# Other buffers' times in a planner, a shared first unit, and a new order of work, in a kernel that mixes a gated unit with a long convolution

## The chip, the cores and the metric

The kernel runs on one core of a Trainium2 chip. The core has a matrix engine (PE in the profile; PEld are its weight loads), a vector engine (DVE), a scalar engine (ACT), a general engine (POOL) and SyncE (SP), which here only issues transfers. Transfers (DMA) move data between the chip's large memory and the on-chip buffer; matmuls write their results into eight small banks, from which DVE and ACT read. Every engine works its own list of instructions in order, and waits where an instruction needs what another engine or a transfer has not finished.

The metric is the device time of one execution in microseconds (us), the median of the runs. A forecast of "no change" means within 0.2%, about 1.25 us here.

## The reference

`x` is 2048 rows by 512 channels. Two branches are computed from it and mixed row by row by a gate:

```python
g = sigmoid((x * gate_w).sum(-1, keepdims=True))
# branch a: a convolution over the 2048 rows, one kernel K per channel, from 128 complex modes
P = exp(dt * A [:, :, None] * l);  K = einsum("dn,dnl,dn->dl", C, P, dt * B).real
a = irfft(rfft(x padded to 4096) * rfft(K padded to 4096))[:2048] + x * Dskip
# branch b: a gated unit, 512 -> 1792 -> 512
b = (sigmoid(x @ w_gate) * (x @ w_up)) @ w_down
out = g * a + (1 - g) * b
```

## The kernel before

**Branch b** is most of the matmul work. The rows are worked in two halves of 1024, each half in two blocks (`sb`) of 512 rows; the 1792 columns in 14 tiles (`f`) of 128, and the tiles in four groups of 3, 4, 4 and 3. Each number is split in two parts, a rounded one (written by ACT, L868) and what is left (written by DVE, L869), and three products of parts stand for one product of full precision. One *unit* (`hidden`) is one `f` for one block: a gate matrix (`k` = 0) and an up matrix (`k` = 1), each with 4 slices (`dc`) of the 512 channels times 3 products, so 12 matmuls of 128x512 into one bank `gups`, 24 in a unit. Sigmoid (ACT), product (DVE) and a split follow (`post`); `down` multiplies by w_down into banks `dps`, three matmuls for each `f`. In the first half the weights are split once and written back to memory (`wsp<-gu`, `wsp<-dnw`), and in the second half they are read from there (`gu<-wsp`, 1 MB; `dnw<-wsp`, 512 KB). Sums over groups are added in memory-to-buffer transfers that POOL issues (`acc<-part`).

**Branch a** is made of many small matmuls. `rows` reads x (`u`), computes the gate, and takes the first step of the transform of x: matmuls `ups`, stored as `a_u`. `steps` computes dt = exp(log_dt) for all channels with 22 small DVE instructions (L326 to L347) on the tile `steps`; `preludes` (tiles `dt`, `pg`), `bases` and `tables` build on DVE and ACT the tables `T` and `B` for 16 groups of 32 channels; their product (`kps`, 64 matmuls that the profile counts as 128) is K. Its transform (`wps`) is evacuated by ACT to `kev` and stored as `a_k`, by 256 channels each (`a_k0`, `a_k1`). Then `passes` runs over frequencies: for each 256 channels eight passes, each of which loads a table `wwu`, then `au<-a_u` and `ak<-a_k` (two transfers of 256 KB each, in short pieces), multiplies (`s2u`, `s2k`; `ustep`, `kstep`), forms the complex product on DVE, multiplies back (`ips`; `inverse`) with a table `wwv`, evacuates to `ev` and stores it (`b_s<-ev`). After the eighth pass `finals` reads `b_s` back (`b_in`) for the last step (`fps`; `last`).

**The early buffers.** Constants and `rows` use a pool of buffers called early: among them `wu`, `gwb`, `steps`, the row tiles, and three of the eight staging buffers `st` (the list `more`), through which all split data comes. When `rows` is done this pool is closed, and the buffers of the passes (pool `fin`: `wwu`, `wwv`, `big` for `au` and `ak`, `uf`, `t`, `ev`, `al`) take the same place in the on-chip memory. An instruction that writes such a buffer waits on the chip until the last user of what lay there is done.

**What sets the order.** Nothing is scheduled by the hardware. Each of the parts above is a Python generator that yields the next piece of work, and `Plan.run` interleaves them into one list. The string `ORDER` tells whose turn it is, a letter for each piece (letter h, for instance, is "hidden PE"); a turn that is not ready is owed and taken as soon as it is. What is ready, and which of several free buffers is taken, follows from the plan's own estimates of time: `Plan.cost` for engines; for a transfer by SP the size at 280 KB a us, a fixed part, and a slack (`SLACK["dma"]`, 1.6 us). A `Slot` is a buffer with the time at which the plan holds it free, an `Ev` an event with such a time. These numbers order the work and choose buffers; the waits on the chip follow from the data.

Around the change stand these lines:

- L323 loads log_dt into `steps`; L316 is every constant's load (`pw`, `gwb`, `wu` and others); L864 loads a piece of x (`st<-xt`) or of weights (`st<-wgu`, `st<-wdn`), L868 and L869 split it.
- L947 are the matmuls of `hidden`, L999 those of `down`, L688, L713 and L751 are `s2u`, `s2k` and `ips`.
- L653, L658, L667 and L671 load `wwu`, `au`, `ak` and `wwv`; L766 stores `b_s`.
- `first_w` is a pair of events that make the loads of the first unit take turns: x's slice 0, the gate weights, x's slices 1 to 3, and only then the up weights.

Of the kernel before, what the change touches and what calls it, by code (L numbers as in the profile page):

```python
# [31 lines left out]
P = 128  # L32
L, D, F, NS = 2048, 512, 1792, 128
NM = L // P
NF = F // P
NC = D // P
# [23 lines left out]
    "HJ0zKI56HJzKHJKh4HJhKIQI56hhhhh8zHI56IhhhIHij0JKHQH56ihhJK56h3h3JK569JijKj2hh7ij1y2VVyWPhQh8ijOhhU8VhNijhi9UMPj9UkUyLUVR"  # L60
    "kklhPURhiYOg7YIh5ffikNMIYY6YYjkPLRPONghgklhYhRjgMTg5ikkPLPhVik7VWTIY56hhUYVTjlhUIihkhUkkYYYUYjiYRYONRMPLP3OYN5MPUZIyLTSX"
    "jlkkRhjVTU6iIYgk6PYOhYh55hYbceQNYTYSfj7fgihglRjkaig8kbMkYb!jIhgVlVhiP6YLWUhhhbTPONbVYYkYY9Y5UYYYZi6kMPUTRRUhjILUVPXkj3hh"
    "T!UYi7lOTjY5iYYgYIfjYYfYhRbRNkgTIg7gcYkhQij8hMPe9LPO6kYQ5hgijTRR5hViT6ablhYNbh8hVWbUMPYTbLVhiPkONhhYUYYMTjh!RUYP9kZjXUUT"
    "ViL6UYgRkijjYhhbcQ89kf2Peh!dT6fggOYg1lkkkkgRRiajNlkkYkkib2YYVhbIhhiYMPIVh5YlbkkW5UT6YVbYLUTPONMUPUYRTYL6UYYYYhojRRVoUk7k"
    "IlIRZXbjiYg5fhckjekh7PkYYYkflaoYkYYkohk5YYikYggghbgbhbblVVWU7kI5jhhYiVihUYYYYkYkUUkUoTjIjZXTlk6hiVU6iYh5gffYYjdkIhYYQO8k"
    "Yh6YNMPLYhihhPONRYRjhgiggbgVjVWUk9TMhioYj!yPLhhQ8VYIPcl9eiTRRaYONYk6hh!jQ89!YUQYMih8jTkUbYZXUiPUjjb9iVjb7UYk!YkgLYbYTY5P"
    "lIShYbcfkShkY6hYkefgggkg35oIaYViOoh5lkkVWUk5N6MPT7khIbbVh!7YYhUbiTlkkYYkYYYZLUU6jX6SUVbj5bkl6U!cehYg3RhijkkY2fkhYY12ofTg"
    "YkYlgagkkokkihilkokgdYIboVYYhVbkbWk56UbhVhYYlk!ohUiYUjkToYYjHkYUQUYj8oVkiT9lUZhXQ8jYhgJYYhYQ87bcikYYf9YeaYKHfjog9bbhTkhb"
    "kghibJgl7hHgoJkYVVWkHkYhiUYVlkYojYkKYhYIhYjZUUdpppppUKhUVhpJijiXKQjUCbkYglnYIABBsqppppkYphhceHrYkrHfrfggikrabGYgYhbbjbhY"
    "DEYIYpEhEgVijCHVYWEFJKHABBisqlrhnFprpJhkkUpkVphoprJrihjGUjUDhUnYYYhCKEloEkkJUkYoEYKEFABBYsVUZliqrX!kk3bYgpkYiKp!YrcFfYhe"  # L70
    "rhphjaplfkirYkgYoYpbpjhg3bGbjbDpEEEgYEhCgVVWiiABBQsqrFUVhklrYppprUhFYppQhIhirGYYkUDCEEEYEpFjYhdjjUABYBsqUkrkiiYrnjhpoplV"
    "rFUZhXYbghjY2YhfhckYrYekfYiakYgg12YbgpYlGpgbYhnVbbkVkk!lYDCEpEEYphkkiWUVYAnjEFBBsYFqUiYklpphphjUkpYoZrrprkkrUlXkbckUVGIj"
    "nkUYYDEYgpYYYEEEhlFFYCABnBsqrppYphrkferkpkYfggrpgijIlihahbbGhjbkbDEEEgECphVYAVWYiYUVYiBBUsqrrrQhFhhhrkiUjYFhUQdUYQYGDEEj"
    "EkjhEVijFFUZXYghijhIhbcelYhkfaYYYYYYfYYgYtijYtxkgbithbugtxwubwQhvwhYgYVhvttxtYtxwiwVWUVIwhbYjhiUjZhUvwjvuuijXUtihjhUtxkt"
    "VUYYbklugYYfhvvwwwtvtkYkYYkYYkhfggxhvgwglkktkijVYVkuvxluYvkWUovwwiwkkIcevVtvvokhholYiUoakjUYjkbkYiYYZjbhktUxUVluvUXkkkbk"
    "vbYgYhYYhbYYhYYhYffcYoiYYgeaYgYglkYkgkYIkdbbbbhjhZIliXbkceQokQabbbhbijhjijkdppppphhChihhhjihjihhABBsqprklrrphkpppphppikh"
    "QrGDEpECEpjihEjApBBsqQFhppkhihjrrrrGDiECEEppEjIhjFABBisjqrhohklhkippppokrkrprFpGCDEhEFEpEABBpsqrrrklhkkkwoFjioFCpprABBpI"
    "sjGpqrrrklhirpkpkkpklDEEEpppEpGphpkDEEEEkkpCABBFFsqrrkjrhlIkpkoCApBrBsqGikklrrrhjrphGDEEEEFFpkkkDEoEkplpECEhoABBFsqrihkh"
    "kkrrrjihiFwGDFhFQhhjEEjEEklhhQkkiQFFtjhttijxtxhhkuwutwtthhtvvxxiiwwttwtowtvwjxvohhikktxtxujtuuvvuvvwmkwkkkjotxkkikwkvmuu"
    "jkmwvnnmnvijkkkknmvwwwmknkkkvnwkvvmnvwkmn")  # L80

XLATE = 0
SLACK = dict(dma=1.6, eng=0.06)
FETCH = 6.5

# [184 lines left out]
def body(ctx, tc, xp, xt, prm, ldt, dsk, gw, wgu, wdn, c_wu, c_wf, c_wk, c_wwu, c_wwv, c_pw, out):  # L270
# [573 lines left out]
    def load_x():  # L844
        for half in range(2):
            for sb in range(2):
# [264 lines left out]
```

## Time and profile before

| what | value |
|---|---|
| median of 3 runs | 626.07 us (624.86 to 626.09) |
| the profiled execution: its own time | 625.42 us |
| its span, first to last instruction | 623.7 us |
| PE busy | 608.8 us, 98% |
| DVE busy | 506.4 us, 81% |
| ACT busy | 429.4 us, 69% |
| idle time of PE: 623.7 - 608.8 | 14.9 us |
| moved by DMA | 140.34 MB, 225 GB/s on average |

A row of a timeline is: start and duration in us, engine, line, operation, output<-inputs, shapes, how many instructions were merged into the row, and in brackets how long the engine had been idle and what ended that. A row of the view by stretches gives, for each stretch of time, its length, the busy time of each engine with the number of instructions, the granted clock, the mean busy share of the 16 DMA engines, and the rate in GB/s. The page's "40 slices" cut the span into 40 equal parts of 15.6 us, each digit a busy share in tenths.

### The profile page before, as it was taken

Reading aid. Unit: us, or ns where it says so; the run is one execution under the profiler, and the core shown is the slowest. Engines: PE = TensorE matmul, PEld = TensorE weight load, DVE = VectorE, ACT = ScalarE, POOL = GpSimd, SP = SyncE. Lnnn points to the kernel's source line nnn. Section 1 sums busy time; section 2 is a strip of 40 time slices with the busy share of each in tenths; the row PEclk is TensorE's granted clock in tenths of the full one; section 3 lists DMA queues with packets and bytes.
Section 4 is the critical chain, followed back from the end, with each engine's and each line's share of the span. In section 5 each row is a group of like instructions: output and inputs, shape, how many; then the busy total and the mean of one; then the engine's idle time right before and its main releaser. Section 6 shows DMA issues by size and latency. Waiting matters only on the chain.

```text
span 623.7 us, 16354 instructions
## 1 busy us (share of the span) xinstructions
PE 608.8 (98%) x6816; PEld 461.0 (74%) x6816; DVE 506.4 (81%) x902; ACT 429.4 (69%) x726; POOL 35.1 (6%) x44
## 2 busy tenths in 40 slices
PE   5999999999999999999999999999999999998997
PEld 3877777787777778877776777777787776775775
DVE  5879899999999999999999999998986163663145
ACT  5597988989989798988878687767684233342210
POOL 0000000010100111010110000000201000110000
PEclk9999999999999999999999999999999999999999
DMA  7844866588759498698999678777856999999875
GB/s 226 287 161 122 288 204 200 182 234 272 219 158 292 134 295 255 197 294 239 209 261 281 202 214 211 244 236 227 236 151 180 229 224 264 247 231 235 256 224 178
DMA packets 97161, 140.34 MB, mean 225 GB/s; under 512 B 40000, under 2 KB 65472, under 8 KB 92480
## 3 DMA queue, kind: packets, MB, share of 16 engines
q1 hardware_dynamic: 91328, 128.81, 67.9%
q0 software_dynamic: 5760, 10.49, 10.1%
q8 instruction: 54, 0.88, 0.6%
q14 instruction: 19, 0.16, 0.1%
HBM read 75.31 MB, written 53.48 MB: 207 GB/s over the span
## 4 chain that ended last, share of the span: by engine, by line
PE 87%; DVE 6%; DMA 3%; ACT 1%; SPq 1%; issue 1%; DVEq 0%; ACTq 0%
PE gups L947 45%; PE dps L999 23%; PE kps L527 5%; PE wps L555 3%; PE ups L606 3%; PE fps L801 2%; PE s2u L688 2%; PE s2k L713 2%; PE ips L751 2%; DMA b_s<-ev 1%; DMA ak<-a_k 1%; DMA st<-wgu 1%; SPq L658 1%; DVE uf L725 0%; DVE tt L724 0%
## 5 line engine op out<-in xcount | busy, mean ns | idle before, releaser
L947 PE MATMUL gups<-x,gu 128*128 128x512 f32 x1344 | 332.6, 396 | 7.5 <-ACT gu L868 6.5
L947 PEld LDWEIGHTS gups<-x,gu 128*128 128x128 f32 x1344 | 250.7, 189 | 76.8 <-issue 12.7
L999 PE MATMUL dps<-dnw,h 128*128 128x512 f32 x672 | 175.9, 397 | 0.0
L999 PEld LDWEIGHTS dps<-dnw,h 128*128 128x128 f32 x672 | 123.1, 188 | 35.2 <-issue 9.0
L1024 POOL DMA_DIRECT2D acc<-part x40 | 34.9, 871 | 549.6 <-ACT part L1022 365.9
L970 ACT ACTIVATE h<-sg 128x512 fp32r<-128x512 f32 x56 | 34.9, 627 | 28.5 <-DVE sg L966 28.5
L477 ACT ACTIVATE B<-B 128x32 f32<-128x32 f32 (+2 forms) x96 | 53.3, 669 | 0.4
L971 DVE TENSOR_TENSOR h<-sg,h 128x512 fp32r<-128x512 f32 x56 | 38.3, 685 | 17.7 <-ACT h L970 17.7
L724 DVE TENSOR_TENSOR tt<-s2k,uf 128x512 f32<-128x512 f32 x32 | 21.9, 686 | 35.2 <-PE s2k L713 34.7
L461 DVE TENSOR_TENSOR T<-T,t 128x64 f32<-128x64 f32 (+4 forms) x80 | 46.5, 581 | 1.2
L459 DVE TENSOR_TENSOR t<-T,bz 128x64 f32<-128x64 f32 (+4 forms) x80 | 46.1, 576 | 1.2
L460 DVE TENSOR_TENSOR T<-T,bz 128x64 f32<-128x64 f32 (+4 forms) x80 | 46.2, 577 | 0.0
L966 DVE TENSOR_TENSOR sg<-gups,sg 128x512 f32<-128x512 f32 x56 | 38.0, 683 | 9.5 <-PE gups L947 5.8
L1022 ACT ACTIVATE part<-dps,omg 128x512 f32<-128x512 f32 x40 | 27.4, 684 | 23.6 <-PE dps L999 23.4
L297 ACT ACTIVATE ev<-ips 128x256 f32<-128x256 f32 x64 | 20.0, 387 | 33.4 <-PE ips L751 20.9
L964 ACT ACTIVATE sg<-gups 128x512 f32<-128x512 f32 x56 | 33.6, 601 | 13.2 <-PE gups L947 12.9
L565 ACT ACTIVATE kev<-wps 128x256 f32<-128x256 f32 x64 | 34.8, 643 | 5.6 <-PE wps L555 5.6
L527 PEld LDWEIGHTS kps<-B,T 128*32 128x32 f32 x2048 | 29.4, 110 | 7.4 <-issue 5.0
L527 PE MATMUL kps<-B,T 128*32 128x64 f32 x2048 | 31.9, 220 | 0.3 <-DVE T L461 0.2
L297 ACT ACTIVATE uf<-s2u 128x512 f32<-128x512 f32 x32 | 17.4, 595 | 18.6 <-PE s2u L688 18.5
L430 ACT ACTIVATE af<-ex 128x1216 int32<-128x1216 f32 x16 | 19.6, 1228 | 15.0 <-DVE ex L421 13.4
L431 DVE TENSOR_TENSOR ex<-ex,af 128x1216 f32<-128x1216 f32 x16 | 22.7, 1418 | 0.7 <-ACT af L430 0.5
(85 smaller groups left out, 684.0 us busy)
## 6 DMA issues: line engine op xcount, KB each, us to landing
wsp<-gu SPq DMA_DIRECT2D x14, 1024.0 KB, 6.9
gu<-wsp SPq DMA_DIRECT2D x14, 1024.0 KB, 7.7
acc<-part POOLq DMA_DIRECT2D x40, 256.0 KB, 6.0
a_u<-evu SPq DMA_DIRECT2D x32, 256.0 KB, 4.4
a_k<-kev SPq DMA_DIRECT2D x8, 1024.0 KB, 5.0
au<-a_u SPq DMA_DIRECT2D x32, 256.0 KB, 6.0
ak<-a_k SPq DMA_DIRECT2D x32, 256.0 KB, 6.7
b_s<-ev SPq DMA_DIRECT2D x32, 256.0 KB, 4.1
```

What stands on the lines that cost most here:

```text
L297: copy = lambda eng, out_, in_: A.activation(out_, in_, AF.Copy) if eng == "ACT" else V.tensor_copy(out_, in_)
L459: yield "DVE", dve(n), lambda: V.tensor_tensor(t2, src, sb, op=OP.mult), [t, slot.t]
L460: t = yield "DVE", dve(n), lambda: V.tensor_tensor(dst, src, br, op=OP.mult), [t]
L461: t = yield "DVE", dve(n), lambda: V.tensor_tensor(dst, dst, t2[:, :, ::-1], op=OP.add), [t]
L477: A.activation(B[:, :, 0, 1 << k::2 << k], B[:, :, 0, 1:64 >> k:2], AF.Exp, scale=float(1 << k))
L527: mm(p[32 * jj:32 * jj + 32, s], T[:, ch, c], B[:, ch, c], start=(c == 0), stop=(c == 1), tile_position=(0, 32 * jj), skip_group_check=True)
L947: mm(p, gu[:, a, k, dc], x[:, b, dc], start=(dc + n == 0), stop=(dc == NC - 1 and n == 2))
L966: t = yield "DVE", dve(512), lambda: V.tensor_tensor(sg, pu, sg, op=OP.mult), [t, tu]
L970: t = yield "ACT", act(512), lambda: A.activation(h[:, 0], sg, AF.Copy), [t, hs.t]
L971: t = yield "DVE", dve(512), lambda: V.tensor_tensor(h[:, 1], sg, h[:, 0].bitcast(F32), op=OP.subtract), [t]
L999: mm(p, h[:, a, 128 * s:128 * s + 128], dn[:, b], start=(f == f0 and n == 0), stop=(f == f0 + gn - 1 and n == 2))
L1024: ts = yield "POOL", kb(430), lambda: nc.gpsimd.dma_start(accs[t], part, accum_op=OP.add), [te, begun[t]]
```

## The change

It has four parts.

1. In `passes`, the plan's time of each buffer of `fin` is no longer 0 but the time at which the early buffers are free (the latest of the three staging buffers and of the event "rows"). The instructions that write these buffers are the same.
2. The plan's estimates for the start: transfers issued before 8 us get a slack of 0.3 us instead of 1.6; the loads of `steps`, `pw` and `gwb` are counted as 150, 490 and 560 KB instead of 2, 38 and 256.
3. The first unit takes two banks at once and goes through x's four slices once, for each slice first the three gate matmuls and then the three up matmuls. Before, all 12 gate matmuls came first. The up weights no longer wait in the plan for x's slices 1 to 3 (`first_w` is one event).
4. The string `ORDER`, some 2,440 letters, is replaced as a whole.

```diff
 ORDER = (
-    "HJ0zKI56HJzKHJKh4HJhKIQI56hhhhh8zHI56IhhhIHij0JKHQH56ihhJK56h3h3JK569JijKj2hh7ij1y2VVyWPhQh8ijOhhU8VhNijhi9UMPj9UkUyLUVR"
+    "0zzHJI5KI56hH6hHJJKhhQI5zKhhHJ6yKhhhh89I56HJ0ihIjK56hI56ihhjiHhH3ji3k2142HJKJKVhVJKiQ8WUjQ8hVUyPjhhhiONjijMPLhU7hh9PUOkS"
...
-                end = max(self.dma, end + 0.6) + 1.4 + SLACK["dma"]
+                end = max(self.dma, end + 0.6) + 1.4 + (min(SLACK["dma"], 0.3) if start < 8 else SLACK["dma"])
...
-        t = yield "SP", kb(2), lambda: S.dma_start(x, ldt), []
+        t = yield "SP", kb(150), lambda: S.dma_start(x, ldt), []
...
-        yield more, len(more)
+        free = max(s.t for s in (yield more, len(more)))
...
             fin[n] = slots(fp, n, k, s)
+            for slot in fin[n]:
+                slot.t = max(free, E["rows"].t)
...
-    first_w = Ev(), Ev()
+    first_w = Ev()
...
                     if (half, sb, dc) == (0, 0, 1):
-                        yield first_w[0]
+                        yield first_w
...
-                if (half, sb) == (0, 0):
-                    first_w[1].set(0.0)
...
-                        if (f, k) == (0, 1):
-                            yield first_w[1]
...
+                    if (half, sb, f) == (0, 0, 0):
+                        banks = []
+                        for k in range(2):
+                            bank, = yield GU, 1
+                            banks.append((bank.tile("gups"), bank))
+                        ends = [None, None]
+                        for dc in range(NC):
+                            for k in range(2):
+                                yield wr[0][k]
+                                gu, gs = wr[1]
+                                yield xr[0][dc]
+                                x, xsl = xr[1]
+                                p, bank = banks[k]
+                                ends[k] = t = yield "PE", ("f", 3 * 0.227, 6.02), partial(mms, p, gu, x, k, dc, 1), [
+                                    bank.t, wr[0][k].t, xr[0][dc].t]
+                        pp = [(*b, e) for b, e in zip(banks, ends)]
...
-    for gen, kind in ((steps(), "steps"), (const("pw", pw, c_pw.to_broadcast([P, NA + NP]), kb(38)), "pw"),
+    for gen, kind in ((steps(), "steps"), (const("pw", pw, c_pw.to_broadcast([P, NA + NP]), kb(490)), "pw"),
...
-                      (const("gwb", gwb, gw.to_broadcast([P, D]), kb(256)), "const"), (preludes(), "preludes"), (bases(), "bases"), (tables(), "tables"),
+                      (const("gwb", gwb, gw.to_broadcast([P, D]), kb(560)), "const"), (preludes(), "preludes"), (bases(), "bases"), (tables(), "tables"),
```

Three places show what the new order moves. The listings are of the built programs; "x2" is two equal instructions in a row, and a number behind a name tells buffers apart.

**The start.** SP's first transfers, before:

```order
L864 DMA st_95<-xt 128x512
L323 DMA steps_93<-ldt 16x32
L864 DMA st_97<-wgu 128x512
L864 DMA st_110<-xt 128x512
L864 DMA st_115<-xt 128x512
L316 DMA pw_86<-c_pw 128x75
L864 DMA st_127<-xt 128x512
L864 DMA st_135<-wgu 128x512
```

And now:

```order
L323 DMA steps_93<-ldt 16x32
L864 DMA st_95<-xt 128x512
L864 DMA st_97<-wgu 128x512
L864 DMA st_120<-wgu 128x512
L864 DMA st_119<-xt 128x512
L864 DMA st_133<-xt 128x512
L864 DMA st_126<-wdn 128x512
L864 DMA st_125<-wgu 128x512
L864 DMA st_139<-xt 128x512
```

`steps` now leads, the up weights (`st_120`) stand in front of x's slices 1 to 3 (`st_119`, `st_133`, `st_139`), and `pw` has moved behind them, to the twentieth transfer.

On DVE, the small instructions on `steps` and the second halves of the splits, before:

```order
L330 SCALAR_TENSOR_TENSOR steps<-steps 16x32
L869 TENSOR_TENSOR x<-st,x 128x512
L869 TENSOR_TENSOR gu<-st,gu 128x512
L333 TENSOR_SCALAR steps<-steps 16x32
L334 TENSOR_TENSOR steps<-steps 16x32
L336 SCALAR_TENSOR_TENSOR steps<-steps 16x32 x5
L337 TENSOR_SCALAR steps<-steps 16x32
L869 TENSOR_TENSOR x<-st,x 128x512 x3
```

And now:

```order
L330 SCALAR_TENSOR_TENSOR steps<-steps 16x32
L333 TENSOR_SCALAR steps<-steps 16x32
L334 TENSOR_TENSOR steps<-steps 16x32
L336 SCALAR_TENSOR_TENSOR steps<-steps 16x32 x5
L337 TENSOR_SCALAR steps<-steps 16x32
L869 TENSOR_TENSOR x<-st,x 128x512
L869 TENSOR_TENSOR gu<-st,gu 128x512 x2
L869 TENSOR_TENSOR x<-st,x 128x512
L341 TENSOR_SCALAR steps<-steps 16x32
```

The second group on `steps` (L333 to L337) stood between two splits, and stands ahead of all of them now; behind the first four splits the third group (L341 to L347, nine instructions) follows.

**The passes over the first 256 channels, SP.** From the third pass's table on, before:

```order
L653 DMA wwu_3675<-c_wwu 128x256
L658 DMA au_3691<-a_u_59 128x2x256 x2
L667 DMA ak_3711<-a_k0_60 64x16x64 x2
L1029 DMA acc0_66<-acc_540 128x512
L766 DMA b_s0_62<-ev_3767 64x1024
L920 DMA wsp_65<-dnw_2949 128x1024
```

And now:

```order
L655 DMA wwu_3669<-c_wwu 128x256
L864 DMA st_3496<-xt 128x512
L660 DMA au_3692<-a_u_59 128x2x256
L374 DMA pg_2810<-prm 128x768
L768 DMA b_s0_62<-ev_3605 64x1024
L660 DMA au_3692<-a_u_59 128x2x256
L669 DMA ak_3778<-a_k0_60 64x16x64
L864 DMA st_3695<-xt 128x512
L669 DMA ak_3778<-a_k0_60 64x16x64
```

Before, the table, `au` and `ak` followed each other; now four other transfers (256 + 384 + 256 + 256 KB) stand between them.

**The passes over the second 256 channels, SP.** The second and the third pass, before:

```order
L653 DMA wwu_6377<-c_wwu 128x256
L658 DMA au_6392<-a_u_59 128x2x256 x2
L667 DMA ak_6404<-a_k1_61 64x16x64 x2
L671 DMA wwv_6408<-c_wwv 128x256
L653 DMA wwu_6417<-c_wwu 128x256
L916 DMA dnw_6257<-wsp_65 128x1024
L658 DMA au_6419<-a_u_59 128x2x256 x2
L667 DMA ak_6463<-a_k1_61 64x16x64
L916 DMA dnw_6432<-wsp_65 128x1024
```

And now:

```order
L655 DMA wwu_6333<-c_wwu 128x256
L660 DMA au_6366<-a_u_59 128x2x256
L914 DMA dnw_6229<-wsp_65 128x1024
L914 DMA dnw_6388<-wsp_65 128x1024
L660 DMA au_6366<-a_u_59 128x2x256
L669 DMA ak_6427<-a_k1_61 64x16x64 x2
L673 DMA wwv_6431<-c_wwv 128x256
L655 DMA wwu_6433<-c_wwu 128x256
L660 DMA au_6440<-a_u_59 128x2x256 x2
L669 DMA ak_6443<-a_k1_61 64x16x64 x2
```

Two loads of 512 KB (`dnw`) have moved from the third pass's loads (behind `wwu_6417`) into the second's (ahead of `wwu_6433`).

More of the change, by code (lines that the diff above doesn't have):

```diff
@@ L934, in hidden, with mms @@
                     pp = []
-                    for k in range(2):
-                        yield wr[0][k]
-                        gu, gs = wr[1]
-                        yield xr[0][0]
-                        x, xsl = xr[1]
-                        bank, = yield GU, 1
-                        p = bank.tile("gups")
-                        m = 1 if (half, sb, f) == (0, 0, 0) else 2
-                        for dc0 in range(0, NC, m):
-                            def mms():
-                                for dc in range(dc0, dc0 + m):
-                                    for n, (a, b) in enumerate(((0, 0), (0, 1), (1, 0))):
-                                        mm(p, gu[:, a, k, dc], x[:, b, dc], start=(dc + n == 0), stop=(dc == NC - 1 and n == 2))
-                            yield xr[0][dc0 + m - 1]
-                            t = yield "PE", ("f", 3 * m * 0.227, 6.02 * m), mms, [bank.t, wr[0][k].t, xr[0][dc0 + m - 1].t]
-                        pp.append((p, bank, t))
+                    def mms(p, gu, x, k, dc0, m):
+                        for dc in range(dc0, dc0 + m):
+                            for n, (a, b) in enumerate(((0, 0), (0, 1), (1, 0))):
+                                mm(p, gu[:, a, k, dc], x[:, b, dc], start=(dc + n == 0), stop=(dc == NC - 1 and n == 2))
@@ new lines, in hidden @@
+                    if (half, sb, f) == (0, 0, 0):
[14 more added lines that the diff above has]
+                        pp = [(*b, e) for b, e in zip(banks, ends)]
+                    else:
+                        for k in range(2):
+                            yield wr[0][k]
+                            gu, gs = wr[1]
+                            yield xr[0][0]
+                            x, xsl = xr[1]
+                            bank, = yield GU, 1
+                            p = bank.tile("gups")
+                            for dc in range(0, NC, 2):
+                                yield xr[0][dc + 1]
+                                t = yield "PE", ("f", 6 * 0.227, 12.04), partial(mms, p, gu, x, k, dc, 2), [bank.t, wr[0][k].t, xr[0][dc + 1].t]
+                            pp.append((p, bank, t))
```

42 lines of the change are left out of this document (21 added, 21 removed).

## The prediction

> **What bounds the kernel now.** I read the page's shares first, then who made PE wait, then the start and the passes from the timeline.
>
> ```profile
> span 623.7 us, 16354 instructions
> PE 608.8 (98%) x6816; PEld 461.0 (74%) x6816; DVE 506.4 (81%) x902; ACT 429.4 (69%) x726; POOL 35.1 (6%) x44
> ...
> PE 87%; DVE 6%; DMA 3%; ACT 1%; SPq 1%; issue 1%; DVEq 0%; ACTq 0%
> ```
>
> PE is busy for 98% of the span, and 87% of the chain that ended last is PE's. So a change is worth what it takes from PE's 14.9 us of idle time, or from time in which PE is busy but slow. The view of waits, for PE alone, splits the idle time:
>
> ```profile
> PE gups L947 <- ACT gu L868: 6.5, 1, 6.5
> PE s2u L688 <- ACT ev L297: 2.2, 1, 2.2
> PE gups L947 <- DVE x L869: 0.8, 1, 0.8
> PE s2k L713 <- DMA ak<-a_k: 0.7, 1, 0.7
> PE gups L947 <- ACT sg L964: 0.3, 1, 0.3
> PE kps L527 <- DVE T L461: 0.2, 1, 0.2
> ```
>
> 6.5 us pass before the first matmul, 0.8 soon after; 2.9 are lost in two passes (`s2u`, `s2k`), 0.5 elsewhere; the rest, 4.2, lies behind the last matmul. No other engine is idle enough to be ignored: by stretches, DVE is busy for 242.3 of the 249 us from 156 to 405, and the transfers are saturated around the passes.
>
> ```profile
> 0.00:16.00 16.00, 8.71 (x24) 6.45 (x25) 8.11 (x30) 9.24 (x13) 0.20 (x4) 1.00 0.74 225
> ...
> 156.00:280.00 124.00, 124.00 (x1460) 97.86 (x1466) 121.13 (x202) 111.04 (x174) 12.12 (x14) 1.00 0.77 230
> 280.00:405.00 125.00, 124.13 (x1861) 92.05 (x1846) 121.19 (x212) 98.55 (x168) 5.23 (x6) 1.00 0.86 233
> ```
>
> **The start.** The timeline of the first 14 us (SP's issues, ACT's and DVE's instructions), and PE's rows:
>
> ```profile
> 1.19 0.41 SPq L323 DMA_DIRECT2D steps<-ldt  x1
> 1.66 0.41 SPq L864 DMA_DIRECT2D st<-wgu  x1
> 3.06 0.43 SPq L316 DMA_DIRECT2D pw<-c_pw  x1
> 4.30 0.17 DVE L326 TENSOR_SCALAR steps<-steps 16x32 f32<-16x32 f32 x1 [3.43 <-DMA steps<-ldt]
> 5.79 0.63 ACT L868 ACTIVATE gu<-st 128x512 fp32r<-128x512 f32 x1 [1.04 <-DMA st<-wgu]
> 7.06 0.16 DVE L333 TENSOR_SCALAR steps<-steps 16x32 f32<-16x32 f32 x1
> 7.26 0.63 ACT L868 ACTIVATE x<-st 128x512 fp32r<-128x512 f32 x1 [0.19 <-DMA st<-xt]
> 8.63 1.28 DVE L869 TENSOR_TENSOR x<-st,x 128x512 fp32r<-128x512 f32 x2
> 9.80 0.63 ACT L868 ACTIVATE x<-st 128x512 fp32r<-128x512 f32 x1 [1.91 <-DMA st<-xt]
> 11.75 0.16 DVE L341 TENSOR_SCALAR steps<-steps 16x32 int32<-16x32 f32 x1
> 13.29 0.18 DVE L347 TENSOR_TENSOR steps<-steps 16x32 f32<-16x32 f32 x1
> ```
>
> ```profile
> 6.47 2.08 PE L947 MATMUL gups<-x,gu 128*128 128x512 f32 x4 [6.47 <-ACT gu L868]
> 9.37 6.84 PE L947 MATMUL gups<-x,gu 128*128 128x512 f32 x20 [0.82 <-DVE x L869]
> ```
>
> ```profile
> 9.40:13.40 4.00, 4.00 (x10) 3.13 (x11) 1.00 0.88 320
> 13.80:17.80 4.00, 4.00 (x19) 3.29 (x18) 1.00 0.63 208
> ```
>
> Before, four matmuls use up what is there, then PE waits for x's next slice, whose split stands on DVE behind L333 to L337 (7.06 to 8.63). The first unit's 24 matmuls end at 9.37 + 6.84 = 16.2. Until about 13.4 a matmul takes about 0.42 us (10 in 4.00, two of them cut by the edges), then 0.22: the array speeds up 4.0 us after PE began to work without a pause, at 9.37. `pw` costs 1.7 us of transfer: x's fourth slice came 2.54 us after the third (7.26, 9.80), the third 0.82 after the second.
>
> Now the gate weights are again the third transfer, so they land at 5.8, and the first matmul starts at 6.47 as before. `steps` is issued 0.45 us sooner and lands at about 3.85. DVE does its first two groups at once, 1.0 us (L326 to L330) and 1.6 (7.06 to 8.63), to 6.45, and then four splits of 0.68: x's slice 0 by 7.15, gate weights 7.85, up weights 8.5, x's slice 1 by 9.2; then nine instructions on `steps` (11.75 to 13.47, 1.7 us) to 10.9, slice 2 by 11.6, the next `gu` by 12.3, slice 3 (its load lands at about 9.8, behind seven others without `pw`) by 13.0. PE: matmul 1 at 6.47, 2 at 7.15, 3 at 7.85, then 0.42 each: 4 to 12 end at 12.1, and none waits. If the array speeds up at 13.4 again, three more are slow and nine fast: end at 15.5, 0.7 sooner than 16.2. If it does so 4.0 us after 7.85, the last twelve take 2.8: end at 14.9, 1.3 sooner. I take **-0.9**, nearer the first, since the array's speed-up shows once in this trace; ends are -1.3 and +0.3 (the weights land later than 5.8 by more than the gain).
>
> The Trainium skill (TensorE: Matmul & The Clock Gate, Part 1: The HAM clock gate) says that the array runs at half rate until one window of about 3.4 us of sustained work is over, and that this window runs freely, so that the moment varies by the run. The trace's 4.0 us agrees. By that rule the speed-up could fall anywhere from 11.3 to 14.7, and the term would be an estimated -1.5 to -0.1.
>
> `pw`, now twentieth on SP, is read only together with what DVE makes of `dt` and `pg`, which stand just ahead of it; at worst DVE's tables start 1.7 us later, and DVE has other splits to do then, so 0. The second block's last x slice now stands behind these three; PE needs it after 72 matmuls, at about 15.3 + 48 x 0.23 = 26, some 10 us after DVE's last split above, so 0 as well.
>
> **Fewer changes of shape.** Counted in the listing of PE's instructions, 128x512 matmuls follow a small one 79 times before and 77 now. The chain prices one entry, with six matmuls behind a small one, and without:
>
> ```profile
> 52.50 1.58 PE gups L947 x6
> ...
> 54.78 5.44 PE gups L947 x24
> ...
> 60.90 1.36 PE gups L947 x6
> ```
>
> 1.58 - 1.36 = 0.22, so -0.45 for two, and some more for leaving: **-0.5**, between 0 and -0.6.
>
> **The passes over the second 256 channels.** The chain ahead of the longest wait, and the load of DMA there:
>
> ```profile
> 558.00 9.31 DMA b_s<-ev
> ...
> 567.86 1.37 PE s2u L688 x32
> 569.23 1.22 PE s2k L713 x32
> ```
>
> ```profile
> 300.00:340.00 40.00, 39.34 (x593) 28.62 (x591) 38.77 (x65) 33.48 (x55) 3.47 (x4) 1.00 0.99 244
> 496.00:570.00 74.00, 71.81 (x932) 50.46 (x937) 36.53 (x66) 26.83 (x61) 6.97 (x8) 1.00 1.01 235
> ```
>
> The last pass waits for a buffer (`ev`) whose store of 256 KB took 9.31 us, since all 16 DMA engines are busy (1.01). Its `s2u` and `s2k` take 2.6 us (567.86 to 570.45) where a pass further down takes 1.95 (292.52 to 294.47); with the 2.2 us of idle time 2.8 are lost. The third pass's table waits for the first pass's `s2k`; from there to the last `ak`, the new order has two loads of 512 KB less, moved to where SP waited: 1.05 MB at 235 GB/s is 4.5 us. Over the same stretch PE has 192 matmuls of 128x512 instead of 201 (counted), at 0.227 (5.44 / 24) 2.0 us less, so it arrives 2.0 sooner. 2.8 - 4.5 + 2.0 leaves 0.3 of waiting: -2.5. Some of the moved loads will still be queued, so **-2.2**; ends are -2.8 (all gone) and +2.0 (moving them frees nothing).
>
> **The passes over the first 256 channels.** SP and PE around the third pass:
>
> ```profile
> 296.15 0.32 SPq L864 DMA_DIRECT2D st<-xt  x1
> ...
> 297.59 0.54 SPq L653 DMA_DIRECT2D wwu<-c_wwu  x1
> ```
>
> ```profile
> 292.52 1.09 PE L688 MATMUL s2u<-au,wwu 64*32 64x256 f32 x32
> 293.40 1.07 PE L713 MATMUL s2k<-ak,wwu 64*32 64x256 f32 x32
> ...
> 309.05 1.18 PE L713 MATMUL s2k<-ak,wwu 64*32 64x256 f32 x32
> ```
>
> There is one `wwu` here, so the third pass's loads start when the second's `s2k` is over, at 294.5; SP got to them at 297.59, behind loads and stores that had waited. The third `s2k` took 1.18 instead of 1.07: the loads were just in time. The listing now has 1,152 KB of others among them, 1.18 MB, at 244 GB/s 4.8 us. PE's work between the two `s2k` is the same 54 matmuls. If SP is there at once, the 3.1 us from 294.5 to 297.6 cover part: +1.7. The 0.7 of the fifth pass then mostly goes, since PE comes later: **+1.0**, between -0.8 and +4.8.
>
> **DVE.** At 97% from 156 to 405, it can follow PE's earlier start only if it is earlier itself. In the first 16 us it was idle for 16.0 - 8.1 = 7.9; in my working it idles 3.85 before `steps` and little until 14. So it gains about as much as PE; **+0.3** for what it does not, between 0 and +0.9.
>
> **The plan's times** (part 1 and 2 of the change) issue nothing, and the real waits on the early buffers are in both kernels. They cost 0 by themselves; all they do is in the order above. The small waits (0.3 and 0.2) I leave as they are; a new one like the largest in the middle would cost 2.2.
>
> Sum: -0.9 - 0.5 - 2.2 + 1.0 + 0.3 = -2.3. The profiled execution took 625.42 (span 623.7 and 1.7 around it), so 623.1 for one like it; the median of the three runs is 0.65 above it, and the forecast against it is 626.07 - 2.3 = **623.8**.
>
> **Rivals.** *The passes' transfers are the bound in both places* (slower). For it: DMA shares of 0.99 and 1.01, and PE's two largest waits inside the run. Then moving `dnw` frees nothing, +2.0, and the third pass is late by the full 4.8 less the 0.7 it takes from the fifth, +4.1; with the start's -0.9 and -0.5 this is +4.7, 630.8; half of the 4.8 covered gives 628.4. It decides once the extra loads delay `ak` by more than 3.1 us. Against it: 280 to 300 has slack by the shares of the whole stretch (0.86 against 0.99 in its middle).
>
> *The start's gain is lost on DVE, or the array speeds up late* (no change). If the array speeds up only after six more slow matmuls, the 24th ends at 12.1 + 6 x 0.42 + 6 x 0.23 = 16.0, -0.2; DVE costs 0.9 and the third pass 1.7: -0.2 - 0.5 - 2.2 + 1.7 + 0.9 = -0.3, 625.8. For it: DVE's 97%. Against: DVE's idle time at the start shrinks too.
>
> *All waits go* (faster still): -1.3 - 0.6 - 2.8 - 0.8 = -5.5, 620.6.
>
> **Chances.** My forecast, 621.5 to 624.8: 0.48. All waits go: 0.08. No change: 0.22. Transfers as the bound: 0.22. So faster by over 0.2% (under 624.8) 0.56, within 0.2% (what a measurement can tell from none) 0.22, slower 0.22. The range, leaving out 1 in 10 at each side: 621.0 to 628.6.
>
> **What the new profile would show.** Right: PE's first 24 matmuls end near 15.3 with no wait of DVE's between; no wait of 2 us before the last `s2u`; less than 1.5 us of waits at the third and fifth `s2k`. Wrong: PE waiting for `ak` at the third pass by over 2 us, or for `T` from DVE between 150 and 405 by more than the 0.2 there is now; DMA shares still at 1 with `b_s` taking 9 us and the last pass late. The time falls outside the range only if a new wait of over 5 us appears that none of these rows shows.

## The result

| | changed kernel | kernel before |
|---|---|---|
| median (14 runs each) | 623.77 us (620.96 to 628.05) | 626.06 us (623.44 to 627.10) |
| the profiled execution, its span | 620.96, 619.2 us | 625.42, 623.7 us |

Two runs of the kernel before, of 676.6 and 861.6 us, lie far outside all others and are left out of every number here. The medians differ by 2.3 us, which is what the prediction said (623.8). But the ratio of the runs is 0.9990 with an interval from 0.9971 to 1.0009: the runs of the changed kernel spread more widely than those before, and between the two a change of 0.1% can't be told from none. Two more measurements of the same two kernels gave 0.9978 (0.9955 to 1.0001) and 0.9987 (0.9948 to 1.0025). Over all three the changed kernel's 32 runs have a mean of 624.3 us and the 58 runs of the kernel before 625.5: 1.2 us less; the medians of the same runs are 623.8 and 625.5, 1.8 less. That the first median says 2.3 and the mean 1.2 is the first thing to explain.

The page of the changed kernel, the lines that answer to those shown of before:

```profile
span 619.2 us, 16380 instructions
PE 607.7 (98%) x6816; PEld 460.9 (74%) x6816; DVE 506.8 (82%) x902; ACT 428.4 (69%) x726; POOL 35.2 (6%) x44
...
PE 80%; DVE 14%; ACT 2%; issue 2%; DMA 1%; SPq 0%; DVEq 0%
```

PE's busy time fell by 1.1 us, its idle time by 3.4 (14.9 to 11.5). Who made PE wait:

```profile
PE gups L937 <- ACT gu L868: 6.2, 1, 6.2
PE gups L937 <- ACT sg L979: 0.7, 1, 0.7
PE fps L803 <- ACT kev L565: 0.2, 1, 0.2
```

The 0.8 us at the start, the 2.2 ahead of the last `s2u` and the 0.7 for `ak` are gone; the wait for `sg` has grown from 0.3 to 0.7. The passes over the second 256 channels are as busy with transfers as they were (a DMA share of 1.01, below), and PE's start is one row, where it was two with a wait between:

```profile
6.21 11.13 PE L937 MATMUL gups<-x,gu 128*128 128x512 f32 x38 [6.21 <-ACT gu L868]
```

The view by stretches shows when the array speeds up: from 11 to 12 us PE works on four matmuls in the kernel before (first row) and on six in the changed one (second row).

```profile
11.00:12.00 1.00, 1.00 (x4) 0.81 (x3) 0.97 (x4) 0.92 (x3) 0.00 (x0) 1.00 0.97 363
11.00:12.00 1.00, 1.00 (x6) 0.80 (x5) 1.00 (x3) 1.00 (x3) 0.00 (x0) 1.00 0.52 148
```

The passes over the second 256 channels:

```profile
496.00:570.00 74.00, 73.92 (x904) 51.77 (x909) 41.71 (x75) 27.25 (x62) 6.98 (x8) 1.00 1.01 240
```

In the third pass over the first 256 channels (SP's issues, then PE's rows):

```profile
291.51 0.33 SPq L655 DMA_DIRECT2D wwu<-c_wwu  x1
291.93 0.63 SPq L864 DMA_DIRECT2D st<-xt  x1
...
296.94 0.62 SPq L669 DMA_DIRECT2D ak<-a_k  x1
```

```profile
290.31 1.07 PE L715 MATMUL s2k<-ak,wwu 64*32 64x256 f32 x32
...
306.01 1.07 PE L715 MATMUL s2k<-ak,wwu 64*32 64x256 f32 x32
```

SP issues the pass's table right when the second `s2k` is over (290.31 + 1.07 = 291.4), where before it came 3.1 us after that; the last `ak` is issued at 296.94, nine us ahead of its use, and lands 8.3 us later, 0.8 us ahead of it; the third `s2k` takes its plain 1.07.

The 24 matmuls of the first unit end at 14.2. This one profile would be 4.5 us of gain, twice what the medians show, and it is the fastest of the 14 runs.

### The profile page after: what moved, and what is told of

Its sections match the earlier page's. It is cut to its first block, busy times and chain, and to the rows that moved or that the text cites. A ratio compares the mean times of both kernels' runs of the same rounds, so it can differ in the third digit from the quotient of the medians.

```text
span 619.2 us, 16380 instructions
## 1 busy us (share of the span) xinstructions
PE 607.7 (98%) x6816; PEld 460.9 (74%) x6816; DVE 506.8 (82%) x902; ACT 428.4 (69%) x726; POOL 35.2 (6%) x44
## 4 chain that ended last, share of the span: by engine, by line
PE 80%; DVE 14%; ACT 2%; issue 2%; DMA 1%; SPq 0%; DVEq 0%
PE gups L937 41%; PE dps L1014 23%; PE kps L527 4%; PE ups L606 3%; PE fps L803 2%; PE wps L555 2%; PE s2u L690 2%; PE s2k L715 2%; PE ips L753 2%; DVE uf L727 1%; DVE tt L726 1%; DVE t L459 1%; ACT B L477 1%; DVE T L460 1%; DVE sg L981 1%
## 5 line engine op out<-in xcount | busy, mean ns | idle before, releaser
L979 ACT ACTIVATE sg<-gups 128x512 f32<-128x512 f32 x56 | 33.6, 600 | 14.5 <-PE gups L937 13.7
L434 ACT ACTIVATE af<-ex 128x1216 f32<-128x1216 f32 x16 | 19.6, 1222 | 6.2 <-DVE ex L431 6.0
```

## The experiments

In both kernels ORDER has 2,441 letters, the same ones in another sequence. So parts of the two lists can be joined. Below, `rest(A, B)` is the list A without the letters that stand in B, each left out once for each time it stands there. Listings of the built programs show that with parts 1 and 2 of the change taken back and the new ORDER kept, every engine has the same instructions in the same order: the whole change lies in the first unit (part 3) and in ORDER (part 4).

The runs were made on three chips, each time beside the kernel before on the same chip. On the first, with 12 runs each beside 33: the changed kernel again, the start alone, the end alone, the two loads put back. On the second, 12 beside 35: all but the start, the old end, forty more instructions, the warm array. On the third, 6 beside 11: the start alone a second time and the three runs of the last section.

### The changed kernel again

> The changed kernel unaltered, timed again beside the kernel before. The prediction's sum: 2.3 us less than before (ratio 0.9963). The two profiled executions, 625.42 and 620.96, would give 4.5 us less (0.9929). A rival says that most of the 4.5 us of that pair is chance from run to run (the changed kernel's runs lie between 620.96 and 628.05), and that another profiled execution will show new stalls in other places: then the ratio is between 0.996 and 1.0, and PE's stalls behind the 24th matmul sum to over 5 us instead of the 3.8 of the first profile.

It took 623.22 us (621.49 to 626.81) against 625.33, ratio 0.9978 (0.9955 to 1.0001). Its profiled execution took 626.81, 5.9 us more than the first profile of the same program. The start differs by 0.6 (24 matmuls end at 14.8). Most of the rest is one place, which the first profile does not have. PE there:

```profile
146.59 1.88 PE L527 MATMUL kps<-B,T 128*32 128x64 f32 x118
151.10 0.38 PE L527 MATMUL kps<-B,T 128*32 128x64 f32 x10 [2.63 <-issue]
151.41 2.21 PE L1014 MATMUL dps<-dnw,h 128*128 128x512 f32 x6
153.42 2.60 PE L937 MATMUL gups<-x,gu 128*128 128x512 f32 x6
```

PE stops for 2.6 us in the middle of the fourth `kps`, waiting for nothing that the profile knows ("issue"), and then six matmuls take 2.21 and 2.60 us instead of 1.4. The stretches of this profile, with the granted clock as the third number from the end:

```profile
142.00:146.00 4.00, 4.00 (x16) 1.94 (x16) 4.00 (x6) 3.98 (x5) 0.00 (x0) 1.00 0.06 14
...
152.00:154.00 2.00, 2.00 (x7) 1.58 (x6) 1.97 (x7) 0.49 (x4) 0.00 (x0) 0.57 1.04 310
154.00:156.00 2.00, 2.00 (x7) 1.58 (x6) 1.90 (x8) 1.97 (x6) 0.00 (x0) 0.58 0.97 381
```

So a stop of 2.6 to 2.9 us brings 4 us at a clock of 0.57 on average, another 1.4 us: 4.3 in all. What PE lacked were its own instructions. They come by DMA in transfers of 16 KB on queue q8, 54 in a run, so one for each 256 of the 13,790 instructions that PE records (a matmul and its weight load are two). Between 127 and 147.5 us the first profile has one such transfer (first list), this one none (second list):

```profile
q1 hardware_dynamic: 1188, 3.22, 48.2%
q0 software_dynamic: 432, 0.79, 21.9%
q8 instruction: 1, 0.02, 0.4%
```

```profile
q1 hardware_dynamic: 1070, 3.01, 44.6%
q0 software_dynamic: 432, 0.79, 21.8%
```

In the first profile it starts at 138.5, in this one at 148.6, ten us later, though the transfers were idle from 142 to 146 (a DMA share of 0.06, above). PE stopped after the 2,497th instruction that it recorded, and so it did in each of the three later profiles that have this stop. In all four the transfer started 0.3 us after the last matmul ahead of the stop had begun, when PE had nothing left, and PE went on 2.3 to 2.5 us later.

The runs tell how often. A mean granted clock of 0.997 or less, called the low clock below, marks a run with the slow clock behind such a stop: every one of the five profiles with a slow stretch has it, and no other. For runs without a profile this is inferred. Of the changed kernel's 32 runs in all three measurements, 14 have it (44%), with a mean of 626.4 us; the other 18 have 622.7. Of the 79 runs of the kernel before that list their clock, 14 have it (18%), with 627.6; the other 65 have 625.0. So among runs without the low clock the change gains 2.3 us, and a run with it is 3.7 us longer. This explains the wide spread. It also shows what the median is worth: in the first measurement the two groups have 7 runs each, and the median lies in the gap between them (623.54 and 624.00); in the other two it came out at 623.22 and 625.70. In the kernel before no profile caught a run with the low clock; that it stops, and where, is not shown.

### The start alone, twice

```diff
 the first unit as changed
-ORDER = old
+ORDER = new[:60] + rest(old, new[:60])
```

> The changed first unit and the first 60 turns of the new list, then the old list: behind the first 40 us every engine has the order of the kernel before. By the prediction's term the start is worth -0.9 us (24 matmuls end near 15.3). By the two profiles it is worth -2.0 (they end at 14.2 instead of 16.2, since the array speeds up at 11.0 and not at 13.4). The rival: the gain is given back in the stretch where DVE is busy 97%, from 156 to 405 us, so 0, with new waits of PE for sg or T there of about 2 us in sum.

It took 623.79 us (620.09 to 626.26), ratio 0.9961 (0.9938 to 0.9984), of all runs the ratio that excludes 1 most clearly. Its 24 matmuls end at 14.55, and PE waits nowhere for DVE or ACT by more than 0.2 behind it, so nothing is given back to DVE. On another chip:

> The start alone a second time, beside the changed kernel. It had the best ratio so far (0.9961) and 2 of 12 runs with the low clock. If the start is the part of the change that gains (1.9 us by the profiles) and the new middle loses by its stop what it saves in waits for ak, this is 0.5 to 1.5 us faster than the changed kernel on the same chip. If the middle and the end gain as the prediction said (1.2 and 2.2 less), it is 1 to 2 us slower.

623.77 us, ratio 0.9969 (0.9938 to 1.0001); the changed kernel beside it took 625.7. Both runs together have a mean of 623.6 us, against 625.5 of the kernel before on these two chips: the start is worth 2.0 us (1.7 among runs without the low clock: 623.3 against 625.0). It is all that the change as a whole gains, and 0.7 more than that (the changed kernel had 624.2 on these chips; with 18 runs each this last difference can't be told from none). The rival that the gain is lost on DVE does not hold.

The profile of the second of these runs has a stop as well, far from the fourth `kps` and with the old order in the middle:

```profile
374.74 1.09 PE L690 MATMUL s2u<-au,wwu 64*32 64x256 f32 x30
377.27 0.40 PE L690 MATMUL s2u<-au,wwu 64*32 64x256 f32 x1 [1.45 <-issue]
```

PE waits 1.45 us here behind the 8,385th instruction that it recorded, which is 2,497 and 23 times 256, and the transfer on q8 started at 374.97, 2.3 us before PE goes on. The granted clock stays at 1.00 behind it. So a late transfer is no matter of the new middle alone, and a stop need not show in the clock.

### All but the start

```diff
 the first unit as before
-ORDER = old
+ORDER = old[:60] + rest(new, old[:60])
```

> The old first unit and the first 60 turns of the old list, then the new list: all of the change but its start. By the prediction's terms 0.9 us slower than the changed kernel; by the start's profiles 1.4 to 2.0 slower (24 matmuls end at 16.2 to 16.5 instead of 14.2 to 14.9). PE's stop inside the fourth kps, which two of three profiles of the new order show (2.9 us, and half clock behind it, 4.3 in all), should come as often as there, if the order in the middle brings it (clock of the run below 0.998 in about 4 of 10 runs, against 2 of 10 with the old middle), and less often if the new start does.

625.06 us against 625.24, ratio 1.0003 (0.9971 to 1.0035): by the medians the new middle and the new end together gain nothing, with an interval of some 2 us to either side. The 24 matmuls end at 16.5. The profile has the stop in the fourth `kps`, 2.4 us, this time without the slow clock behind it, and 4 of the 12 runs have the low clock (mean 628.7; the other eight 623.8, where the kernel before has 625.0 without it). So the stop in the fourth `kps` doesn't need the new start.

### The end alone, the old end, and the two loads put back

```diff
-ORDER = old
+ORDER = old[:2002] + rest(new, old[:2002])
```

> The old code and list up to 480 us, then the new order: only the passes over the second 256 channels and what lies behind them change. By the prediction's term -2.2 us: no wait of 2 us before the last s2u. The rival that the transfers are the bound there whatever their order gives 0 or +2.0, with a wait of the same size before another s2u or s2k.

```diff
-ORDER = new
+ORDER = new[:2000] + rest(old, new[:2000])
```

> The changed kernel up to 480 us, then the old order: the counterpart of the end alone. If the new order of the end is worth 2.2 us, this is 2.2 slower than the changed kernel (median near 625.4 where that one's was 623.2), with a wait of about 2 us before the last s2u. If, as the four profiles so far suggest, waits of the passes over the second 256 channels sum to 1.1 to 3.7 us under either order (before 3.1, start alone 2.8; changed 1.2 and 2.1, end alone 3.7), it is within 0.7 us of the changed kernel.

```diff
 SP, passes over the second 256 channels
 wwu (second pass)
-au, dnw, dnw, au, ak, ak, wwv
+au, au, ak, ak, wwv
 wwu (third pass)
-au, au, ak, ak
+dnw, au, au, ak, dnw, ak
```

> The changed kernel, with one thing undone: the two 512-KB loads of dnw stand in the third pass over the second 256 channels again, behind its table and behind its first ak, as before the change. All else on every engine is the same. If these two loads are the cause of the end's gain, as the prediction has it, +1 to +2.2 us against the changed kernel, with a wait of 1 to 2 us before the last s2u or s2k. If the gain comes from the rest of the new order there (192 matmuls instead of 201 ahead of it, stores and loads of gu in other places), 0 within 0.5 us.

The end alone took 624.58 us, ratio 0.9983 (0.9961 to 1.0005); the changed kernel with the old end 623.81, ratio 0.9975 (0.9949 to 1.0001); with the two loads put back 622.99, ratio 0.9969 (0.9943 to 0.9995). The changed kernel itself had 0.9978. Neither undoing costs the 1 to 2.2 us that the prediction's cause asks for, though intervals of 1.4 to 1.6 us to either side can't exclude a cost of 1. The profiles say why: the wait is not a fixed size. How much longer the last `s2u` and `s2k` and the wait ahead of them took than in an undisturbed pass (1.89 us from start to end), in each profile:

| end of the list | us in the last pass | 13th `ips` |
|---|---|---|
| old order | 2.9 (before), 1.9, 0.6, 2.3, 2.9 | no wait in any |
| new order | 0.9 (first profile), 0.9, 0.5, 0, 1.3, 0.6, 1.9, 2.3 | 0.2 to 1.3 in seven of eight |
| new, the two loads put back | 2.5 | no wait |

The new order takes about 1.0 from the last pass on average (2.1 to 1.1) and gives 0.7 of it back at an `ips` that waits for banks, and what a single profile shows can be anything from 0 to 2.9. Passes ahead of the last wait in some profiles too (1.6 us in the fifteenth, with the end alone). All eight passes and their `ips` together lose 0.7 to 3.8 us with the old end (mean 2.5) and 0.1 to 3.9 with the new (mean 2.0). The third row suggests that the two loads decide where the wait falls; it is one profile, and it doesn't show that they decide how much is waited.

### Forty more instructions, and a warm array

```diff
                                start=(c == 0), stop=(c == 1), tile_position=(0, 32 * jj), skip_group_check=True)
+                            if gi == 0 and c == 0 and 4 * s + jj < 10:
+                                mm(p[32 * jj:32 * jj + 32, s], T[:, ch, c], B[:, ch, c],
+                                   start=True, stop=False, tile_position=(0, 32 * jj), skip_group_check=True)
```

> The changed kernel, with ten matmuls of the first kps written twice: 40 more instructions on PE ahead of the fourth kps, 0.3 us of work. Nothing else moves. PE stopped after exactly the same instruction in both profiles with a stop, where the next 256 of its instructions (a transfer of 16 KB on queue q8, 10 us later than in the first profile) had not come. If the place of that boundary inside the fourth kps is the cause, 40 instructions more move it from the kps's last 20 instructions to its middle, PE has some 4.5 us more until it gets there, and the stop becomes rarer or shorter: clock below 0.998 in at most 2 of 12 runs, median 1 to 1.5 us below the changed kernel's. If the late transfer has nothing to do with the place, the share of such runs stays at 4 of 10 and the median rises by 0.3.

625.86 us, ratio 1.0021 (0.9996 to 1.0046): slower than the changed kernel by 2.6, against the expectation. In its profile the fourth `kps` is whole, and PE stops elsewhere, so the place of the boundary counts:

```profile
273.39 1.99 PE L527 MATMUL kps<-B,T 128*32 128x64 f32 x128
275.32 1.08 PE L718 MATMUL s2k<-ak,wwu 64*32 64x256 f32 x29
278.41 0.62 PE L718 MATMUL s2k<-ak,wwu 64*32 64x256 f32 x3 [2.02 <-issue]
278.96 2.58 PE L940 MATMUL gups<-x,gu 128*128 128x512 f32 x6
```

An `s2u`, a `kps` and an `s2k` stand in a row there, 384 instructions in 4 us. In the changed kernel the boundary lies some 35 instructions behind that row; 40 more move it among the last three matmuls of the `s2k`. PE stops after the 5,569th instruction, which is 2,497 and 12 times 256. The transfer starts at 276.2, when PE is already there. 7 of the 12 runs have the low clock. That is not all that they lose: the five runs without it have a mean of 625.3, where the changed kernel's have 622.7. A stop without the slow clock, as with the old start and in the second run of the start alone, would be one reason; no profile of such a run is there to show it.

```diff
+    warm = JU[0].tile("warm", dtype=F32R)
+    V.memset(warm.bitcast(F32), 0.0)
+    wb = XB[3].tile("warmp")
+    for i in range(20):
+        mm(wb[:, :256], warm[:, :128], warm[:, :256], start=True, stop=True)
```

> The changed kernel, with 20 matmuls of 128x256 on a zeroed tile ahead of the first unit, from about 1.5 to 6 us, while PE has nothing to do; they write a bank that nobody reads, and the output doesn't change. They also are 40 more instructions on PE. If the array speeds up some 4.4 to 6.1 us after steady work begins, as the six profiles show, it does so between 6 and 7.6 us here, and the 24 matmuls end at 12.8 to 13.4, bounded by the split of x's last slice (its load lands at 10.3), instead of 14.2 to 14.9: 1.4 us less. With the stop in the fourth kps rarer as in the run before, the median is 2.5 below the changed kernel's, about 620.7. If the speed-up only counts work on real data or comes at a fixed time near 11 to 12 us, nothing is gained.

625.56 us, ratio 1.0020 (1.0000 to 1.0040), with the same stop in the first `s2k`, after the same 5,569 instructions, and the low clock in 9 of 12 runs. What the start does is seen all the same:

```profile
1.49 4.64 PE L581 MATMUL warmp<-warm 128*128 128x256 f32 x20 [1.49 <-DVE warm L578]
6.24 2.35 PE L942 MATMUL gups<-x,gu 128*128 128x512 f32 x7
8.81 1.95 PE L942 MATMUL gups<-x,gu 128*128 128x512 f32 x6 [0.23 <-DVE x L874]
11.04 1.79 PE L942 MATMUL gups<-x,gu 128*128 128x512 f32 x6 [0.28 <-DVE x L874]
13.05 4.15 PE L942 MATMUL gups<-x,gu 128*128 128x512 f32 x17 [0.22 <-DVE x L874]
```

The array is at full speed from 7.3 us, 5.8 after the first matmul on zeros and 1.0 after the first on data, so work on zeros counts. But the unit still ends near 14.5: each slice of x comes from DVE just in time for a slow array, the last at 13.05, where the expected end would need it by 12.0 (13.4 - 6 x 0.23). With the slow array most of this was hidden; by this profile the start has little left to give.

### The fourth kps later

```diff
 PE
+dps x3
+dps x3
 kps (the fourth)
-dps x3
-dps x3
```

> The changed kernel, with one thing moved: two groups of three dps matmuls stand ahead of the fourth kps instead of behind it. The instructions of the other engines are the same. PE's boundary of 256 instructions lies 12 instructions earlier in the fourth kps, and PE reaches it 1.4 us later. If the stop is a race between the transfer of PE's next 256 instructions and the fourth kps, runs with a clock below 0.998 fall from about 4 of 10 to at most 2 of 12, or the stop gets 1.4 us shorter; DVE, which waits for the fourth kps, may lose up to 1.4 us in each run. Median 0 to 1.5 us below the changed kernel's. If the stop is something else, the share stays.

> The changed kernel unaltered a third time, so that the next three stand beside it on one chip. By the runs so far: ratio to before 0.996 to 1.000, about 4 of 10 runs with a granted clock below 0.998. If its profile is one with a stop, it stops behind the same instruction of the fourth kps as in the two profiles that had one.

> The start alone, with six gups matmuls ahead of the fourth kps instead of behind it: 12 instructions and 1.4 us more for PE's next instructions to come. If the 1 or 2 of 10 low-clock runs with the old middle are the same stop, they go too, and the median falls by up to 0.5 us against the start alone; if not, the same within 0.3.

Six runs each: the changed kernel 625.70 (ratio 0.9987, 0.9948 to 1.0025; 3 with the low clock, and the profile has the stop at the same instruction, 2.5 us), with `kps` later 624.48 (0.9984, 0.9950 to 1.0019; 1 with the low clock), the start alone with six `gups` ahead of the fourth `kps` 625.32 (0.9981, 0.9948 to 1.0015; none, as in the start alone beside it). Six runs are too few to tell these shares apart. The profile of the second has no stop at the fourth `kps`; but its transfer started at 138.7, about as early as in the profiles that have none with the order unchanged, so whether the move is the reason is not shown. What it costs is:

```profile
145.19 0.96 PE L1014 MATMUL dps<-dnw,h 128*128 128x512 f32 x3
147.77 1.66 PE L1014 MATMUL dps<-dnw,h 128*128 128x512 f32 x6 [1.61 <-ACT part L1037]
149.36 1.99 PE L527 MATMUL kps<-B,T 128*32 128x64 f32 x128
```

The moved `dps` need a bank that ACT has not emptied yet, and PE waits 1.6 us for it, where the stop and the slow clock cost up to 4.3 in some of the runs.

## Why the prediction was right, and where only its sum was

The median is the predicted one, 623.77 for 623.8, a small gain at the edge of what can be told, and that it fell there is luck: it lies in a gap between two groups of runs. The terms that make up the sum did not hold.

**The start, -0.9: right in kind, too small.** PE's start has no wait in it in the changed kernel's three profiles, as said. The 24 matmuls end at 14.0 to 14.9 in ten profiles with the new first unit and no warming, and at 16.2 to 16.5 in three with the old one: -2.0 on average, confirmed by the time of the start alone, and outside the term's bound of -1.3. The step that failed is "nearer the first, since the array's speed-up shows once in this trace". In the profiles with the new start the speed-up comes 3.5 to 6.1 us after the first matmul, so at 9.8 to 12.4 and never as late as 13.4; in the old it comes at 13.7 to 14.7 (13.7 in the profile of before, where I had read 13.4), which is 4.4 to 6.2 us after the wait of 0.7 to 0.8 is over. So the wait seems to start the count again, which no run tries by itself. I had counted from 7.85, when I thought that PE's waits for DVE would be over; behind the first matmul at 6.2 there were none of over 0.15 us until the array was fast. The Trainium skill (TensorE: Matmul & The Clock Gate, Part 1: The HAM clock gate) says that a free-running window of about 3.4 us has to be filled with work, from which one would estimate 3.4 to 6.8 us behind the first matmul; the 3.5 to 6.1 of the ten profiles agree with it.

**The passes over the second 256 channels, -2.2: wrong.** Two loads less in the third pass were to take the last pass's wait away. The end alone is 0.7 us faster than the kernel before by the means (624.7 for 625.4, and its ratio's interval includes 1); the old end and the loads put back, which should have been slower than the changed kernel, have ratios 0.0003 and 0.0009 below its own, 0.2 and 0.6 us, which is within the noise. The wait itself varies: with the same order at the end the last pass loses 0.6 to 2.9 us (old) or 0 to 2.3 (new). The step that failed is the first: the 2.8 us that "are lost" were one draw, and I took them for the price. The rival "moving them frees nothing" is the nearer one here, without its loss in the third pass.

**The passes over the first 256 channels, +1.0: wrong in sign.** The extra 1.18 MB lie among the loads, as said, but SP is there at once, where before it came 3.1 us after the table's buffer was free, and the last `ak` is issued nine us before it is read (seven before the change) and lands 0.8 us before. No profile with the new middle has a wait for `ak` of over 0.5 us in the third or fifth pass. The step that failed is that the 3.1 us "cover part" and leave +1.7: they covered all of it, but with little to spare: over the nine profiles with the new middle the last `ak` of the third pass lands between 2.2 us before the third `s2k` starts and 0.2 after.

**DVE, +0.3: too small.** It is not `T` that comes late but `uf`, the complex product: in all nine profiles with the new middle the eighth `ips` is 0.6 to 0.7 us longer, since its weight loads wait 0.4 to 0.5 us for DVE. In the first profile:

```profile
395.52 0.42 DVE L733 TENSOR_TENSOR uf<-tt 128x256 f32<-128x256 f32 x1
396.00 0.64 PEld L753 LDWEIGHTS ips<-uf,wwv 32*64 32x64 f32 x24 [0.51 <-DVE uf L733]
```

With the wait for `sg`, which ACT writes (0.3 to 0.7 us instead of 0.2 or 0.3), this is up to 1.1 us, about what the middle saves in waits for `ak`.

**Fewer changes of shape, -0.5, and the plan's times, 0.** The second holds by the listings (the same program without them). The first was not tried by itself; it is inside the 0 of all but the start.

**What was missing: PE's own instructions.** The new middle raises the share of runs with the low clock, which the profiles tie to a stop for them. Over the kernels whose middle is new and whose PE instructions there are those of the changed kernel, 28 of 68 runs have the low clock (44% in the changed kernel's own), with the old middle 17 of 115 (18% in the kernel before). With 3.7 us between the two groups of the changed kernel (626.4 and 622.7), 26 in 100 more runs cost 1.0 us of the mean. Counted in runs without the low clock, on the two chips that have both, the start gives -1.7 and all else -0.5 (622.8 for the changed kernel); with +1.0 for the stops this is -1.2, as the means differ. The -0.5 is what is left over, so this is a split and no proof of it. None of my rivals had it, and "issue" stood in the page of before only as a share of 1%.

That the sum came out is chance: the start gains 0.8 to 1.1 us more than its term, all else in runs without the low clock about 0.9 less than its terms (-0.5 for -0.5 - 2.2 + 1.0 + 0.3 = -1.4), and half of the first 14 runs, not more, had the low clock, so that their median fell between the groups.

Open is why the transfer of instructions is late in some runs and early in others of the same program. At the fourth `kps` it starts 5 to 6.5 us before PE is through what it has in all five profiles with the old middle; with the new one, unshifted, it was 7 to 9 us early in two and too late in four. In the profiles with a stop there the transfers were idle for part of the time in between, and no row says what it waited for.

## What to carry to other kernels

A wait in one profile is one draw: where transfers are at their limit, look at a second and a third profile of the same program before a wait of 2 us is taken for what its removal brings, and look at the runs' spread and clocks before the medians. A start can be priced by when the array's speed-up may come, here 3.5 to 6.1 us after steady work begins, and by whether a wait of PE's falls before it. In a program with hundreds of tiny matmuls in a row, PE can outrun the transfers that bring its instructions: count 256 to 256 from one stop, see whether other stops lie whole multiples away, and look at the time of the transfer ahead of each. A short way between two boundaries alone doesn't tell: 256 instructions passed in 2.6 us without a stop in the run with forty more instructions, and the stop of the start alone came after 6.8 us.

## What had not been expected of the hardware

- PE's program came in transfers of 16 KB, one for each 256 instructions. The seven stops in fourteen profiles lie after 2,497, 5,569 and 8,385 recorded instructions, whole multiples of 256 apart, and PE went on 2.2 to 2.5 us after the transfer had started. With the new middle PE goes from one boundary to the next in 4.2 to 4.4 us at the fourth `kps`, and stopped there for 2.4 to 2.7 us in four of six profiles; with the old one in 4.0 us in four profiles and 5.2 in the fifth, and did not stop, so the length alone does not decide. 40 instructions more moved the stop 130 us down the program.
- A stop that short was enough to bring the half clock: a granted 0.50 for 3.4 us behind five of the six stops of 2.0 to 2.7 us in the view of waits, and none behind the sixth (2.4) nor behind the seventh (1.4). The Trainium skill (TensorE: Matmul & The Clock Gate, Part 1: The HAM clock gate) names an idle window of about 3.4 us for that; here less did it, perhaps since the tiny matmuls ahead of the stop fill little of the array, which no run tells apart.
- Twenty matmuls on zeros sped up the array like work on data: full speed 5.8 us after the first of them.
